# Threshold attention and a bilinear feed-forward layer: separate PSUM banks for scores in the first nine slots, and weight conversions split around the other work

## The chip, the cores and the metric

The kernel runs on one core of a Trainium2 chip. The metric is the device time of one execution in microseconds (us). A core has a matrix engine (PE, with its weight loads shown apart as PEld), three engines for elementwise work (DVE, ACT and POOL), and SP, which here only issues DMA transfers. Each works through its own list of instructions in order and waits for the others by semaphores. PE writes its results into PSUM, which this kernel uses as four pairs of banks; DVE and ACT read them from there.

## The reference

```python
scores = scale * np.matmul(q, k.transpose(0, 1, 3, 2))
thresh = np.max(scores, axis=-1, keepdims=True) - tau
scores = np.where(scores >= thresh, scores, -1000000000.0)
scores = scores - np.max(scores, axis=-1, keepdims=True)
attn = np.exp(scores)
attn = attn / (np.sum(attn, axis=-1, keepdims=True) + 1e-09)
x = concat_heads(np.matmul(attn, v))       # (8*576, 512)
...
a = x @ w_a
b = x @ w_b
return (a * b @ w_out).astype(np.float32)
```

There are 8 batches, 8 heads, 576 rows and a head width of 64; q, k and v are float32. The feed-forward part (below: ffn) has 4608 rows, width 512 and inner width 1536. Its three weight matrices arrive as 64-bit floats, 18.9 MB in all, and the kernel turns them into float32 itself.

## The kernel before, in words

**Slots.** The attention is cut into 160 units of up to 128 query rows for a pair of heads: `(i, u)`, pair `i` and row tile `u`, where `u = 4` is the tail of 64 rows of both heads. The program is a written-out loop over slots `g` (L756 to L837). Slot `g` computes the scores of unit `g` (`scores`, L314), their row maxima (`mx`, DVE L332), a bias (POOL L334) and a threshold (POOL L336), the exponentials (ACT L364), the masked product with its row sums (DVE L367), and the reciprocals (L376 to L380). Between these it places work of earlier units, of the weights and of the ffn. `keep_order` (L38) pins the order of emission on every engine, so what is written earlier in a slot runs earlier on its engine.

**The first eight units** (`BY_PE = 8`) are pairs 0 to 3 with row tiles 0 and 1. They are normalised and transposed on PE: `diagonals` (L388) makes a diagonal matrix `dg` of the reciprocals on ACT, and `turn_pe` (L396) in the next slot multiplies by it, in one large product (L406, evacuated by ACT L408) and a small one (L412, evacuated by DVE L414). In slots 2 to 9 `weighted_unit` (L499) multiplies with `v` (`pv`, L479), joins the two halves (ACT L468, DVE L469) and copies them for the ffn (POOL L489). In slots 0 to 2, q and k of the next pair are transposed on PE and copied out by DVE (L312). Later units are normalised on ACT (L386), transposed on DVE (L433, L446) and sent through DRAM (L441, L453, L464).

**Weights.** There are 36 pieces of 128 x 512 words of 64 bits (12 each for `wa`, `wb` and `wo`). `load_weights` (L193) has SP load them, at most `RAWS = 4` into work buffers and some more into the still unused `sums_u` space. Each then goes through two ACT instructions (L225, L226, `convert_first`), a POOL clamp (L232), and in the next slot a DVE sign (L238), a DVE shift (L246) and a POOL add (L251). `early[g]` lists the pieces whose first part is in slot `g`: two for slots 0 to 3, three for slots 4 to 9, two for slots 10 to 14. All signs, all shifts and all adds of a slot are placed together ahead of the masked products.

**The ffn** is a generator (`ffn`, L553) that goes through blocks of 256 rows. A block takes 24576 columns of moving data for `a` and `b` (L578, groups named `pab`, evacuated by ACT L584 for `a` and DVE L586 for `b`) and 12288 for the output (L665, or fewer by L621 once sums of weights are ready); 36864 in all is `BLOCK_COLS`. `advance(cols)` (L699) emits that many columns and may stop in the middle of a group, whose PSUM pair then stays taken. A planner sets `cols` per slot: `PACE_EARLY * BLOCK_COLS` up to slot 8, later what the backlog needs before the next block arrives, which is at slot 20 for the second block. In slots 0 to 8 it is all emitted at the slot's end, after the conversions; later in four portions. The first block has to wait for its rows and for `state["converted"]`, which must be 8, 16 and 24 before its inner steps 0, 2 and 4 (each step is two groups).

**PSUM.** `banks` (L125) takes any free pair of the four. The `h` buffers hold both the ffn's products and `dg`; the `osb` buffers hold the low parts of pieces in conversion.

Of the kernel before, what the change touches and what calls it, by code (L numbers as in the profile page):

```python
# [10 lines left out]
FP32 = mybir.dt.float32  # L11
# [11 lines left out]
PV_LAG = 4  # L23
# [6 lines left out]
CATCH_UP = 0.05  # L30
PACE_EARLY = 0.04
ROOM = 1024
# [19 lines left out]
def kernel(  # L52
# [62 lines left out]
    def pool(name, bufs, **kw):  # L115
        return ctx.enter_context(tc.tile_pool(name=name, bufs=bufs, **kw))
# [5 lines left out]
    scratch = pool("scratch", 3, space=bass.MemoryType.DRAM)  # L122
    psum = pool("psum", 4, space=PSUM)

    def banks(n, name):  # L125

        return psum.tile([P, 2, 512], FP32, tag="banks", name=name)[:, :, 0:n]

# [55 lines left out]
    raws, stages, extra, taken = {}, {}, [], {}  # L184
    state = {"loaded": 0, "converted": 0, "rows": 0, "sums": False, "through": 0, "over": False}

# [61 lines left out]
    def convert_add(n):  # L248
        if n in stages:
            top, low = pieces[n][0].bitcast(I32), stages.pop(n).bitcast(I32)  # L250
            nc.gpsimd.tensor_tensor(top, top, low, op=ALU.add)  # L251
            state["converted"] += 1

# [134 lines left out]
    def diagonals(i, u):  # L388

        ws, rcp = weights[i, u]  # L390
        dg = work.tile([P, 2, P], FP32, tag="h", bufs=H_BUFS, name="dg")
        for j in range(2):
            nc.scalar.activation(dg[:, j], ident, AF.Copy, scale=rcp[:, j:j + 1])
        weights[i, u] = (ws, dg)
# [88 lines left out]
    def x_tile(name):  # L483
        return work.tile([P, HP, HALF], FP32, tag="xT", bufs=XT_BUFS, name=name)
# [14 lines left out]
    def weighted_unit(i, u):  # L499

        b, hp = pairs[i]
        pv = product(turned.pop((i, u, "pe")), loaded[i]["v"], P)
        if (b, 0) not in x_of:
            x_of[b, 0] = x_tile("xT")
            state["xs"] = x_tile("xS")
        join(x_of[b, 0][:, hp, u * P:(u + 1) * P], pv[:, 0], pv[:, 1])
        exchange(x_of[b, 0], state["xs"], hp, u * P, (u + 1) * P, nc.gpsimd)
        if hp == HP - 1:
            state["rows"] = u + 1
            if u == 0:  # L510
                blocks.append(((x_of[b, 0], state["xs"]), ("first", b, 0)))

# [186 lines left out]
    def advance(cols):  # L699
        running["owed"] += cols  # L700
        while running["owed"] > 0:
# [13 lines left out]
            else:  # L715
# [4 lines left out]
                running["room"] = min(ROOM, whole // 2)  # L720

    def make_room():

        while running["rest"] and not (running["done"] >= running["room"] <= running["rest"]):
            owed = running["owed"]
            running["owed"] = 0.0
            advance(1)
            running["owed"] += owed - 1
# [7 lines left out]
    for i in range(0, NPR, HP):  # L736
# [7 lines left out]
    arrivals = [g + PV_LAG + 1 for g, (i, u) in enumerate(units)  # L744
                if i % HP == HP - 1 and part(i, u) and (i >= HP or u == NT - 1)]
    first = {i: g for g, (i, u) in enumerate(units) if u == 0}

    for name in ("q", "k"):
        prep_copy(*prep_pe(0, name))
    early = {}  # L750
    n = 0
    for g in range(NPIECES):
        size = min(3 if 4 <= g < 10 else 2, NPIECES - n)
        early[g] = list(range(n, n + size))
        n += size
    for g in range(len(units) + PV_LAG):  # L756
        written = len(pending)
        here = g < len(units)
        converting = bool(early.get(g)) or bool(early.get(g - 1))
# [4 lines left out]
        exchange_blocks()  # L764
        pace = (PACE if g > BY_PE else PACE_EARLY) * BLOCK_COLS
        if g > BY_PE:
            pace = min(pace, backlog() / (min([a for a in arrivals if a > g] + [len(units) + PV_LAG + 1]) - g))
# [4 lines left out]
        if g < 3:  # L772
            prep_copy(*prep_pe(g + 1, "q"))
        for n in early.get(g - 1, []):
            convert_sign(n)
        for n in early.get(g - 1, []):
            convert_shift(n)
        for n in early.get(g - 1, [])[-1:] + early.get(g - 1, [])[:-1]:
            convert_add(n)
        if g == 3:  # L780
            for c in range(0, NSUM - 2 * CW + 1, 2 * CW):
                extra.append(sums_u32[:, c:c + 2 * CW].rearrange("p (f w) -> p f w", w=2))
        load_weights(RAWS)
        if g > BY_PE and g <= len(units):
# [3 lines left out]
        if here:  # L788
            weigh(i, u)
        if 0 < g <= BY_PE:  # L790
            turn_pe(*units[g - 1])
# [13 lines left out]
        for n in early.get(g, [])[:1]:  # L805
            convert_first(n)
            convert_clamp(n)
        if here:
            reciprocal(i, u, nc.scalar if converting else nc.vector)
        if here and g < BY_PE:  # L810
            diagonals(i, u)
        elif here:
            normalise(i, u)
        for n in early.get(g, [])[1:]:
            convert_first(n)
            convert_clamp(n)
        load_weights(RAWS)
        for p in range(HP, NPR):
# [57 lines left out]
```

## Time and profile before

| what | value |
|---|---|
| median of 3 runs | 1483.64 us (1479.65 to 1484.49) |
| profiled execution | 1480.79 us, of which the span from first to last instruction is 1478.9 us |
| PE, PEld busy | 1425.3 us (96%), 1201.8 us (81%) |
| DVE, ACT, POOL busy | 925.8, 669.7, 360.1 us |
| first `sc` matmul of slots 0 to 4 | 11.79, 18.44, 26.44, 36.03, 43.17 us |
| ... of slots 5 to 10 | 49.47, 61.29, 70.65, 79.71, 90.87, 103.73 us |
| ... of slots 11 to 16 | 112.93, 122.50, 129.84, 138.74, 147.49, 157.16 us |
| ... of slots 17 to 20 | 164.14, 171.13, 176.39, 182.91 us |

The busy share of PE is taken from modelled ends of pipelined matmuls[...]. The starts of slots are read from the timeline of PE: the first `sc` matmul of each unit. A wait in the timeline stands in square brackets behind an instruction: how long its engine was idle before it, and whose end released it. The figure behind "x" is the number of records; a float32 matmul has two records here, so one inner step of the ffn over 64 rows of weights has eight.

### The profile page before, as it was taken

Reading aid. Unit: us, or ns where it says so; the run is one execution under the profiler, and the core shown is the slowest. Engines: PE = TensorE matmul, PEld = TensorE weight load, DVE = VectorE, ACT = ScalarE, POOL = GpSimd, SP = SyncE. Lnnn points to the kernel's source line nnn. Section 1 sums busy time; section 2 is a strip of 40 time slices with the busy share of each in tenths; the row PEclk is TensorE's granted clock in tenths of the full one; section 3 lists DMA queues with packets and bytes.
Section 4 is the critical chain, followed back from the end, with each engine's and each line's share of the span. In section 5 each row is a group of like instructions: output and inputs, shape, how many; then the busy total and the mean of one; then the engine's idle time right before and its main releaser. Section 6 shows DMA issues by size and latency. Waiting matters only on the chain.

```text
span 1478.9 us, 57127 instructions
## 1 busy us (share of the span) xinstructions
PE 1425.3 (96%) x25344; PEld 1201.8 (81%) x25344; DVE 925.8 (63%) x2068; ACT 669.7 (45%) x1213; POOL 360.1 (24%) x563
## 2 busy tenths in 40 slices
PE   5777999999999999999999999999999999999998
PEld 4666587898879898898888788889888888888886
DVE  5767677778767776675645766577756766622212
ACT  4766355555544554553533544355444554411010
POOL 3876522204030312122222213130404040310000
PEclk9999999999999999999999999999999999999999
DMA  9957888789868976786547876588756976530000
GB/s 192 214 154 184 169 168 191 175 178 194 209 139 169 193 174 144 176 184 163 125 118 137 183 164 150 119 188 184 158 138 138 193 174 158 135 90 16 2 17 16
DMA packets 624582, 220.75 MB, mean 149 GB/s; under 512 B 542928, under 2 KB 612048, under 8 KB 624336
## 3 DMA queue, kind: packets, MB, share of 16 engines
q1 hardware_dynamic: 621968, 216.52, 66.8%
q8 instruction: 199, 3.26, 0.9%
q10 hardware_dynamic: 2368, 0.59, 0.2%
q14 instruction: 47, 0.39, 0.1%
HBM read 127.40 MB, written 89.65 MB: 147 GB/s over the span
## 4 chain that ended last, share of the span: by engine, by line
PE 86%; DVE 5%; DMA 3%; ACT 2%; SPq 2%; issue 1%; POOL 1%; ACTq 0%; DVEq 0%; POOLq 0%
PE pab L578 47%; PE po L621 19%; PE sc L325 10%; PE pv L479 10%; PE po L665 1%; DVE tw L433 1%; DVE low L238 1%; DVE mx L332 1%; DMA swap<-tw 1%; DVE tw L367 1%; DMA raw<-in_moe_w_b_dram 1%; SPq L206 1%; SPq L151 0%; SPq L441 0%; DMA sums_u<-in_k_dram 0%
## 5 line engine op out<-in xcount | busy, mean ns | idle before, releaser
L332 DVE TENSOR_REDUCE mx<-sc 128x1 f32<-128x576 f32 x288 | 205.1, 749 | 133.0 <-PE sc L325 122.2
L578 PE MATMUL pab<-xS,wa_sb 64*64 64x256 f32 (+1 forms) x3584 | 271.6, 371 | 0.9 <-POOL xS L489 0.9
L578 PE MATMUL pab<-xS,wb_sb 64*64 64x256 f32 (+1 forms) x3584 | 268.2, 372 | 0.0
L325 PE MATMUL sc<-kT,qT 64*64 64x288 f32 x2304 | 243.4, 413 | 19.2 <-DVE kT L312 8.1
L590 POOL TENSOR_TENSOR h<-h 128x256 f32<-128x256 f32 x168 | 117.4, 733 | 542.1 <-PE po L621 539.0
L578 PE MATMUL pab<-xT,wa_sb 64*64 64x256 f32 (+1 forms) x3200 | 237.6, 371 | 5.3 <-POOL thr L336 2.1
L578 PE MATMUL pab<-xT,wb_sb 64*64 64x256 f32 (+1 forms) x3200 | 235.2, 368 | 5.6 <-DVE h L586 4.1
L621 PE MATMUL po<-wo_sb,h 64*64 64x256 f32 x3264 | 240.1, 376 | 0.0
L386 ACT ACTIVATE tw<-tw,rcp 128x576 f32<-128x576 f32 x244 | 176.1, 768 | 130.1 <-DVE rcp L380 129.9
L364 ACT ACTIVATE tw<-sc,bias,scalars 128x576 f32<-128x576 f32 x260 | 214.7, 832 | 38.3 <-POOL bias L334 25.4
L578 PEld LDWEIGHTS pab<-xS,wa_sb 64*64 64x64 f32 x3584 | 192.4, 133 | 31.3 <-POOL xS L489 5.3
L367 DVE SCALAR_TENSOR_TENSOR tw<-sc,thr,tw 128x576 f32<-128x576 f32 x260 | 203.6, 802 | 20.7 <-ACT tw L364 19.8
L578 PEld LDWEIGHTS pab<-xS,wb_sb 64*64 64x64 f32 x3584 | 193.6, 134 | 25.2 <-issue 0.8
L621 PEld LDWEIGHTS po<-wo_sb,h 64*64 64x64 f32 x3264 | 176.0, 132 | 24.8
L578 PEld LDWEIGHTS pab<-xT,wa_sb 64*64 64x64 f32 x3200 | 170.4, 134 | 30.4 <-DVE kept L469 4.3
L578 PEld LDWEIGHTS pab<-xT,wb_sb 64*64 64x64 f32 x3200 | 169.6, 133 | 27.9 <-DVE h L586 4.5
L479 PE MATMUL pv<-wT,vm 64*64 64x320 f32 (+3 forms) x2592 | 187.2, 381 | 3.1 <-ACT h L584 1.6
L325 PEld LDWEIGHTS sc<-kT,qT 64*64 64x64 f32 x2304 | 143.3, 135 | 52.5 <-issue 14.4
L621 PE MATMUL po<-sums_u,h 64*64 64x256 f32 x2448 | 180.6, 376 | 0.0
L433 DVE STREAM_TRANSPOSE tw<-tw 128x576 f32<-128x576 f32 x240 | 171.6, 753 | 0.2 <-ACT tw L386 0.2
L586 DVE TENSOR_TENSOR h<-h,pab 128x512 f32<-128x512 f32 (+1 forms) x112 | 73.3, 655 | 147.9 <-PE pab L578 140.1
L479 PEld LDWEIGHTS pv<-wT,vm 64*64 64x64 f32 x2592 | 141.6, 135 | 26.3 <-issue 2.8
(85 smaller groups left out, 1236.9 us busy)
## 6 DMA issues: line engine op xcount, KB each, us to landing
swap<-tw SPq DMA_DIRECT2D x240, 288.0 KB, 5.2
wT<-swap SPq DMA_DIRECT2D x28, 1440.0 KB, 7.8
wT<-swap SPq DMA_DIRECT2D x32, 1152.0 KB, 6.3
vm<-in_v_dram SPq DMA_DIRECT2D x32, 288.0 KB, 4.8
qT<-in_q_dram SPq DMA_DIRECT2D x112, 72.0 KB, 3.6
kT<-in_k_dram SPq DMA_DIRECT2D x112, 72.0 KB, 5.1
swap<-wt SPq DMA_DIRECT2D x112, 72.0 KB, 2.7
out_dram<-kept SPq DMA_DIRECT2D x30, 256.0 KB, 4.5
```

Of the source, the lines that this page charges most:

```text
L206: engine.dma_start(dst, part)
L325: nc.tensor.matmul(sc[j if u < NT else 0][to, c], qT[r, q0:q0 + D], kT[r, c * SH:(c + 1) * SH], start=True, stop=True)
L332: nc.vector.tensor_reduce(mx[:, c], sc[j], axis=AX.XY, op=ALU.max)
L364: nc.scalar.activation(wb[j], sb[j], AF.Exp, bias=bias[:, j:j + 1], scale=e_scale)
L367: nc.vector.scalar_tensor_tensor(out=wv, in0=sb[j], scalar=thr[:, j:j + 1], in1=wv, op0=ALU.is_ge, op1=ALU.mult, accum_out=sums[:, j:j + 1])
L386: nc.scalar.activation(w, w, AF.Copy, scale=rcp[:, j:j + 1])
L433: nc.vector.transpose(w, w)
L479: nc.tensor.matmul(pv[j * D:(j + 1) * D, r], vm[rows, k0], wT[rows, k0], start=(s == (NT if j == r else 0)), stop=(s == NT - 1))
L578: nc.tensor.matmul(pab[c * D:(c + 1) * D, r], w[rows, f // n, k, fs + c * D:fs + (c + 1) * D], moving, start=(k == 0), stop=(k == H - 1))
L586: nc.vector.tensor_tensor(ht, ht, pab, op=ALU.mult)
L590: (nc.vector if state["over"] else nc.gpsimd).tensor_tensor(*a, **kw)
L621: nc.tensor.matmul(po[c * D:(c + 1) * D, r, y], ht[rows, t0:t0 + D], other[rows, f], start=(f == 0), stop=(f == NF // 2 - 1))
```

## The change

- **Banks.** The four pairs get a tag each. Up to slot 8 (`state["apart"]`) scores alternate over pairs 0 and 1, and everything else over pairs 2 and 3, where one that an unfinished ffn group holds is left out. From slot 9 on all four are taken strictly in turn.
- **Conversions.** `convert_rest(g, k)` does sign, shift and add of one piece. Piece 0 of the slot before stays ahead of the masked products, piece 1 follows the normalisation, and piece 2 follows the ffn part (in slots up to 8). The `converted` counter the ffn looks at is that of the end of the previous slot.
- **Order.** In slots up to 8 the ffn part comes before the first halves of pieces 1 and 2, and `finish_group` carries it on to the end of its group. The reciprocal of the first eight units is placed straight behind the masked products, wholly on DVE.
- **Sizes.** Three pieces per slot from slot 4 to the end, so the last first half is in slot 13. `PACE_EARLY` is 0.06. From slot 9 on at most two pieces are loaded into work buffers. `dg` comes from the `osb` buffers. The changes in `weighted_unit` and `arrivals` give the same order of work for these units.

```diff
-PACE_EARLY = 0.04
+PACE_EARLY = 0.06
...
-    psum = pool("psum", 4, space=PSUM)
+    psum = pool("psum", 1, space=PSUM)
+
+    state = {"loaded": 0, "added": 0, "converted": 0, "rows": 0, "sums": False, "through": 0, "over": False,
+             "apart": True, "own": 1, "other": 1, "bank": 3, "last": 3, "held": None}
     def banks(n, name):
-        return psum.tile([P, 2, 512], FP32, tag="banks", name=name)[:, :, 0:n]
+        if state["apart"]:
+            own = name == "sc"
+            state["own" if own else "other"] ^= 1
+            if not own and 2 + state["other"] == state["held"]:
+                state["other"] ^= 1
+            m = state["own"] if own else 2 + state["other"]
+        else:
+            m = state["bank"] = (state["bank"] + 1) % 4
+        if name in ("pab", "po"):
+            state["last"] = m
+        return psum.tile([P, 2, 512], FP32, tag=f"banks{m}", name=name)[:, :, 0:n]
...
-            state["converted"] += 1
+            state["added"] += 1
...
-        dg = work.tile([P, 2, P], FP32, tag="h", bufs=H_BUFS, name="dg")
+        dg = work.tile([P, 2, P], FP32, tag="osb", bufs=OSB_BUFS, name="dg")
...
+    def finish_group():
+        left = None
+        while running["rest"] and running["left"] != left:
+            left, owed = running["left"], running["owed"]
+            running["owed"] = 0.0
+            advance(1)
+            running["owed"] += owed - 1
+        state["held"] = state["last"] if running["rest"] else None
...
+    def convert_rest(g, k):
+        for n in early.get(g - 1, [])[k:k + 1]:
+            convert_sign(n)
+            convert_shift(n)
+            convert_add(n)
...
-        size = min(3 if 4 <= g < 10 else 2, NPIECES - n)
+        size = min(2 if g < 4 else 3, NPIECES - n)
...
+        state["converted"] = state["added"]
+        if g == BY_PE + 1:
+            state["apart"], state["bank"] = False, state["last"]
+        if g == BY_PE + 2:
+            running["owed"] = 0.0
...
-        for n in early.get(g - 1, []):
-            convert_sign(n)
-        for n in early.get(g - 1, []):
-            convert_shift(n)
-        for n in early.get(g - 1, [])[-1:] + early.get(g - 1, [])[:-1]:
-            convert_add(n)
+        convert_rest(g, 0)
...
-        load_weights(RAWS)
+        load_weights(RAWS if g < 9 else 2)
...
             weigh(i, u)
+        if here and g < BY_PE:
+            reciprocal(i, u, nc.vector)
...
-        if here:
-            reciprocal(i, u, nc.scalar if converting else nc.vector)
         if here and g < BY_PE:
             diagonals(i, u)
         elif here:
+            reciprocal(i, u, nc.scalar if converting else nc.vector)
             normalise(i, u)
+        convert_rest(g, 1)
+        if g <= BY_PE:
+            advance(pace)
+            finish_group()
+        convert_rest(g, 2)
         for n in early.get(g, [])[1:]:
             convert_first(n)
             convert_clamp(n)
-        load_weights(RAWS)
+        load_weights(RAWS if g < 9 else 2)
...
-        advance((PORTIONS[2] if g > BY_PE else sum(PORTIONS[:3])) * pace)
-        advance(PORTIONS[3] * pace)
+        if g > BY_PE:
+            advance(PORTIONS[2] * pace)
+            advance(PORTIONS[3] * pace)
```

More of the change, by code (lines that the diff above doesn't have):

```diff
@@ L184 @@
     raws, stages, extra, taken = {}, {}, [], {}
-    state = {"loaded": 0, "converted": 0, "rows": 0, "sums": False, "through": 0, "over": False}
     NSUM = NF // 2 * 3 * CH
@@ L502, in weighted_unit @@
         pv = product(turned.pop((i, u, "pe")), loaded[i]["v"], P)
[L503 to L508, printed above, removed]
+        h, c0 = u // 2, u % 2 * P
+        if (b, h) not in x_of:
+            x_of[b, h] = x_tile("xT"), x_tile("xS")
+        x, xs = x_of[b, h]
+        join(x[:, hp, c0:c0 + P], pv[:, 0], pv[:, 1])
+        exchange(x, xs, hp, c0, c0 + P, nc.gpsimd)
+        if hp == HP - 1 and h == 0:
             state["rows"] = u + 1
             if u == 0:
-                blocks.append(((x_of[b, 0], state["xs"]), ("first", b, 0)))
+                blocks.append(((x, xs), ("first", b, 0)))
+        if hp == HP - 1 and u == NT - 1:
+            blocks.append(((x, xs), ("half", b, h)))
     def weighted(i, h):
@@ L743 @@
             units += [(p, u) for p in range(i, i + HP) for u in (2, 3, NT)]
-    arrivals = [g + PV_LAG + 1 for g, (i, u) in enumerate(units)
+    arrivals = [g + (PV_LAG if g >= BY_PE else 2) + 1 for g, (i, u) in enumerate(units)
                 if i % HP == HP - 1 and part(i, u) and (i >= HP or u == NT - 1)]
@@ L764 @@
         exchange_blocks()
-        pace = (PACE if g > BY_PE else PACE_EARLY) * BLOCK_COLS
-        if g > BY_PE:
+        pace = (PACE if g > HP * 2 else PACE_EARLY) * BLOCK_COLS
+        if g > HP * 2:
             pace = min(pace, backlog() / (min([a for a in arrivals if a > g] + [len(units) + PV_LAG + 1]) - g))
```

## The prediction

> **What bounds the kernel now.** I read the page's busy shares and slices first: PE is 96% busy, but its first four slices stand at 5 to 7 tenths. Then the table of stages.
>
> ```profile
> core 0: us, PE busy (x) PEld busy (x) DVE busy (x) ACT busy (x) POOL busy (x), PEclk, DMA share, GB/s
> 0.00:157.00 157.00, 116.32 (x2116) 95.91 (x2120) 107.94 (x238) 99.03 (x185) 100.52 (x142) 0.92 0.81 183
> ...
> 400.00:600.00 200.00, 198.10 (x3515) 174.34 (x3509) 137.94 (x315) 99.31 (x179) 48.33 (x77) 1.00 0.76 168
> ```
>
> From 157 us on (slot 16) PE has almost no gaps: in each 200 us up to 1400 it is busy 198 to 200. Work kept from PE before 157 us is never caught up, so the end moves by what the start of slot 16 moves. Up to then no engine is full: DVE, POOL and ACT are each busy 99 to 108 of 157 us and PE 116. The time lies in waits between them, so next came the timeline of all engines in slots 8 and 9.
>
> ```profile
> 80.86 0.66 ACT L226 ACTIVATE low<-sums_u 128x512 f32<-128x512 uint32 x1
> 81.42 0.35 ACT L584 COPY h<-pab 128x256 f32<-128x256 f32 x1
> 81.83 0.70 PE L325 MATMUL sc<-kT,qT 64*64 64x288 f32 x4 [0.98 <-ACT h L584]
> ...
> 88.05 0.44 PE L412 MATMUL tp<-dg,tw 128*64 128x128 f32 x4 [1.22 <-ACT wT L408]
> ...
> 93.28 0.35 ACT L584 COPY h<-pab 128x256 f32<-128x256 f32 x1
> ...
> 93.68 1.20 PE L479 MATMUL pv<-wT,vm 64*64 64x128 f32 x34 [1.61 <-ACT h L584]
> ...
> 100.36 1.10 PE L578 MATMUL pab<-xT,wb_sb 64*64 64x128 f32 x32 [2.67 <-DVE h L586]
> ```
>
> Two of the eight score products of slot 8 stop until ACT has evacuated an ffn group (L584), which stands behind four conversions on ACT. The small transpose product waits for the large one's evacuation: scores hold two pairs, a half-done ffn group a third, one is left. In slot 9 `pv` and then the ffn wait the same way. The POOL timeline shows how full that engine is, and that a 128x2 operation can take 0.30 us or five times that:
>
> ```profile
> 55.03 1.54 POOL L336 TENSOR_SCALAR thr<-mx,scalars 128x2 f32<-128x2 f32 x1
> ...
> 64.26 0.30 POOL L336 TENSOR_SCALAR thr<-mx,scalars 128x2 f32<-128x2 f32 x1
> 67.65 2.53 POOL L251 TENSOR_TENSOR wb_sb<-wb_sb,low 128x512 int32<-128x512 int32 x2 [1.70 <-DVE wb_sb L246]
> 70.14 1.29 POOL L251 TENSOR_TENSOR wa_sb<-wa_sb,low 128x512 int32<-128x512 int32 x1
> ```
>
> **What the Trainium skill says.** "Perfetto Trace Analysis", Optimization Strategy: repeated bubbles on the engine that should be full can mean that PSUM or SBUF lacks room for the next tile. The L412 row agrees; the wait of 1.22 us recurs at 67.83, 76.89 and 88.05. "PSUM — Partial Sum Buffer", Engine vs sequencer instructions: the queues of ScalarE, VectorE and GpSimd are strict FIFO and matmuls start and end in program order. So it is at 81.42. "SBUF — State Buffer", Who interferes with whom: a VectorE instruction with two SBUF inputs, or in a two-port mode, locks GpSimd out. The two `thr` rows fit it: 1.54 us beside DVE signs and shifts (54.28 to 57.2), 0.30 otherwise. The change leaves those instructions in being, so I allow 0.4 us per slot for it.
>
> **The change, part by part.** An ffn inner step over 128 columns takes 0.875 us per 32 records (L578 at 105.67, 106.55, 107.42), that is four steps, 512 columns: 1.71 ns a column. A half-width group is 1024 columns, 1.75 us.
>
> *Slots 5 and 8.* The planner's columns rise from 0.04 x 36864 + 576 - 640 = 1411 to 0.06 x 36864 + 576 - 640 = 2148, and `finish_group` rounds that up to three groups. Slot 5 does three; slot 6 only one, since step 2 needs 16 pieces and the counter, now a slot late, has 11 then and 14 in slot 7, which does none; slot 8 (17) does three. Seven groups in place of 5644 / 1024 = 5.5. On PE slot 5 is scores 1.2 + `pv` 1.2 + transposes 2.05 + 0.44 + three groups 5.25, and some 0.6 for the ACT evacuation (L408) before the first group: 10.7 us. Scores of the next slot wait for no group any more. The late conversions on ACT (4 x 0.57 = 2.3 us) run beside the next scores (1.2) and maximum (0.7) and bias (0.3); without that cover they would cost 2.3.
>
> *Slots 6 and 7.* PE has 5 to 7 us, ACT 7.5, DVE 7.4; POOL is longest: adds 2.53 + 1.29, clamps 3 x 0.62, bias and threshold 0.9, copies 1.3 = 7.9, plus the 0.4: 8.3 us. The next bias queues behind the last two clamps, and the exponentials wait for it; DVE has piece 0 (0.64 + 0.34 us) to do meanwhile.
>
> *Slot 9.* The waits of 1.61 and 2.67 us go, since no group is open and ACT's group copies come before its conversions. DVE: maxima 1.42, join 0.25, three pieces 3.0, transposes 1.35, products 1.5, ffn and small ones 0.6 = 8.1; POOL 8.3; with a hop I take 9.0.
>
> Slots 5 to 9 together: 10.7 + 8.3 + 8.3 + 10.7 + 9.0 = 47.0 against 103.73 - 49.47 = 54.3: **-7.3 us**. The 1.5 groups done ahead (2.6 us of PE) I count at nothing: the planner spreads the first block up to slot 20 anyway. Were PE the limit in slots 10 to 15, they would be a gain.
>
> *Slots 1 to 4* (31.0 us). One sign and shift (1.0 us) now stand behind the masked products, and in slots 1 to 2 behind the copy of k that the next scores wait for; the add of 1e-9 moves from ACT, behind conversions, to DVE (0.16 in place of 0.20 and two hops of 0.25). DVE is otherwise full in slot 4. Some 0.5 + 1.2 + 0.6 + 0.2: **-2.5 us**. With two pairs for the five other products, each waits only for the second last one's evacuation. Bounds 0 and -4.
>
> *Slots 10 to 15* (53.4 us). Slots 10 to 12 get one more first half each (ACT 1.15, POOL 0.62), and 11 to 13 one more second half (DVE 1.0, POOL 1.27): I take +1.0 in all, since the masked products no longer queue behind three pieces. Slots 14 and 15 lose two second halves each but one: -3. Sum **-2**, bounds +5 and -6. SP's loads: fewer in flight (2 plus the four in `sums_u`), each issued at the sign of the piece six before, so about one slot of 9 us ahead against 3.9 to 7.0 us to landing. SP's swap transfers (4.4 us of issue) stand between; late pieces of `wo` need one issue of 0.33. I cost it at nothing; if that cover fails, a piece is some 2 us late.
>
> *Banks in turn, slot 9 on.* The trace has no row for it. Zero if the pair in turn is always free, else PE waits. At 604.85 scores start, their first pair is read to 611.04 (L367): 6.2 us. In turn it is needed after scores 1.0, a full group 3.46 and `pv` 2.4, 6.9 us. The margin is thin but positive: **+1 us**, bounds 0 and +20. It can't gain, as PE idles only 5 us there (the waits of PE after 200 us).
>
> `dg` from `osb`: five buffers for at most four live tiles, nothing.
>
> Sum: -7.3 - 2.5 - 2 + 1 = **-10.8 us**. The profiled span of 1478.9 becomes 1468, the execution 1470; the median lies 2.85 above the profiled execution, so I predict **1473 us**.
>
> **The rivals.** *Slower: the strict turn costs more than the start gains.* In 151 slots from slot 9 on, scores hold their pairs for about 6.2 us with 0.7 to spare. Where a short tail unit, a late DVE or an output group of 3072 columns that just ended meets its own pair, PE stops for some tenths, up to 1.5 us for an evacuation. From 15.3 / 151 = 0.10 us per slot on, the change is slower by over 0.3%; at 0.12 the time is 1473 - 1 + 18 = 1490. For: the pool of before may take any free pair and PE has no slack. Against: two groups between reuses are nearly always there. Chance 0.15. *Slower by late pieces:* in slots 9 to 13 three pieces come through six places, and six of them late by 2 us cost 12, with slots 10 to 13 at DVE's and ACT's limit (+5) it ends near 1487 to 1490. Chance 0.09.
>
> *No change:* The same DVE, POOL and ACT work remains, and if POOL's late clamps and port locks keep a slot of three pieces near 10 us, only the waits of slot 9 go: -3 us, 1481. For: 9.4 of 10 us of POOL in the stretch 50 to 60. Chance 0.14.
>
> *Larger gain:* slots 5 to 13 run at 8.5 us, 14 and 15 at 7: 76.5 + 14 = 90.5 against 107.7, with -2.5 ahead, -20 us: 1464. For: no engine has more than 8.3. Against: PE has 10.7 in two of them. Chance 0.12.
>
> **How the numbers follow.** The likeliest case, 6 to 16 us gained, has 0.50; its own range is 1468 to 1478. Some 0.3%, 4.5 us, is what this measurement can tell from no change. Faster: 0.50 + 0.12 = 0.62; same 0.14; slower 0.15 + 0.09 = 0.24. The range from 1461 to 1490 takes in most of the larger gain and half of the slower cases, and leaves out 0.05 below and 0.12 above.
>
> **What would show it.** Right: slot 10's first scores near 94 us in place of 103.73 and slot 16's near 146; no wait of scores for ACT L584 or of L412 for L408 up to slot 8; PE busy 198 of 200 us from 200 to 1400 as before. Wrong: new PE waits for DVE L367, `kept` or `osb` evacuations after 200 us (strict turn); ACT L225 waiting for DMA (late pieces); POOL full with 10 us slots (no change).

## The result, and the profile after

| | before | after |
|---|---|---|
| median | 1484.07 us (1479.65 to 1485.25, 4 runs) | 1591.89 us (1591.46 to 1595.04, 4 runs) |
| ratio to before | | 1.0737 [1.0711, 1.0763] |
| profiled span | 1478.9 us | 1589.3 us |
| PE busy, PEld busy | 1425.3, 1201.8 us | 1458.5, 1166.8 us |
| mean granted PE clock | 0.991 | 0.974 |

The kernel became 7.4% slower, where 1473 us was predicted. Lines in the changed file are 12 to 15 higher: `mx` L344, bias L346, exponentials L376, masked products L379, `tp` L418 and L424 with copies L420 and L426, joins L480 and L481, `pv` L491, `pab` L593 with evacuations ACT L599 and DVE L601, `po` L636, sign, shift and add L250, L258, L263.

First the table of stages of the kernel after, with the same columns as before (busy time and records of PE, PEld, DVE, ACT and POOL, then PE's granted clock, the DMA share, GB/s):

```profile
core 0: us, PE busy (x) PEld busy (x) DVE busy (x) ACT busy (x) POOL busy (x), PEclk, DMA share, GB/s
0.00:157.00 157.00, 111.70 (x2060) 92.97 (x2064) 116.56 (x238) 95.14 (x175) 96.29 (x139) 0.92 0.79 181
...
400.00:600.00 200.00, 178.12 (x3021) 139.38 (x3015) 121.40 (x274) 88.27 (x159) 33.98 (x56) 0.96 0.69 148
```

The start did not get denser: PE is busy 111.7 us of the first 157, before 116.3. And from 400 to 600 us, where of all the edits only the turn is still at work, PE is busy 178 of 200 us in place of 198, it works off 3021 records in place of 3515, and its clock is 0.96 in place of 1.00. Scores of slot 20 start at 190.82 us (before 182.91), so 7.9 us are lost up to there. From there to the end of the span it takes 1398.5 us against 1296.0: **102.5 of the 110.4 us are lost after slot 20**.

Next PE's list of waits from 200 us on; these are its six largest rows. Before, the sum of this list was below 6 us (2.1 us for `kept`, 2.0 for issue, and smaller ones).

```profile
PE po L636 <- DVE kept L481: 19.5, 6, 5.4
PE pab L593 <- ACT h L599: 15.9, 9, 3.1
PE pab L593 <- DVE h L601: 13.7, 4, 4.7
PE po L636 <- DVE sums L390: 9.4, 3, 3.9
PE pab L593 <- DVE kept L481: 5.6, 3, 4.2
PE po L636 <- DVE h L601: 4.0, 1, 4.0
```

The figures are the sum in us, the number of waits and the longest. In these rows 26 waits make 68 us, mean 2.6; the rest of the list is nine waits of `pv` (6.3 us) and two of scores (1.0 us). Every waiting group in the rows shown belongs to the ffn, and nearly every releaser is the evacuation of an ffn group: `h` of `pab`, `kept` of `po`. `DVE sums L390` is a 128x2 operation that can release no PSUM pair; where it is named, it only came last in time. The timeline of all engines at 350 us shows one of these waits:

```profile
350.11 1.42 DVE L445 STREAM_TRANSPOSE tw<-tw 128x576 f32<-128x576 f32 x2
351.05 0.83 ACT L376 ACTIVATE tw<-sc,bias,scalars 128x576 f32<-128x576 f32 x1
351.46 0.77 DVE L379 SCALAR_TENSOR_TENSOR tw<-sc,thr,tw 128x576 f32<-128x576 f32 x1
351.78 0.58 ACT L480 COPY kept<-po 128x512 f32<-128x512 f32 x1
352.17 0.81 DVE L379 SCALAR_TENSOR_TENSOR tw<-sc,thr,tw 128x576 f32<-128x576 f32 x1
352.90 0.77 DVE L309 STREAM_TRANSPOSE kT<-kT 128x576 f32<-128x576 f32 x1
353.60 0.64 DVE L481 TENSOR_TENSOR kept<-kept,po 128x512 f32<-128x512 f32 x1
```

PE had ended the output group `po` at 349.4 us. Its evacuation is a copy on ACT and then an add on DVE. The copy stands behind the exponentials and starts 2.4 us later; the add stands behind swap transposes, masked products and a transpose of the next k, and ends at 354.2. The next `po` group is in the pair that this add has just read, and starts at 354.30. So one start in the pair of the group just ended costs not one evacuation (0.58 + 0.64 us) but all that ACT and DVE have queued ahead of it: 4.93 us.

The idle time is not all. Here is PE's own timeline after four waits (us from the start, duration of the group, and in brackets the wait and its releaser):

```profile
354.30 5.40 PE L636 MATMUL po<-wo_sb,h 64*64 64x256 f32 x48 [4.93 <-DVE kept L481]
441.37 2.82 PE L636 MATMUL po<-wo_sb,h 64*64 64x256 f32 x48 [1.81 <-DVE kept L481]
466.93 1.96 PE L593 MATMUL pab<-xT,wb_sb 64*64 64x256 f32 x32 [3.07 <-ACT h L599]
494.35 3.69 PE L593 MATMUL pab<-xT,wa_sb 64*64 64x256 f32 x32 [4.69 <-DVE h L601]
```

48 records of one shape take 2.82 us after a wait of 1.81, and 5.40 us after one of 4.93; 32 records of another shape take 1.96 us after 3.07 and 3.69 after 4.69. The table of stages after the first of these waits has PE's clock in its third column from the right:

```profile
354.30:358.00 3.70, 3.70 (x36) 2.26 (x40) 0.18 (x2) 1.44 (x2) 0.72 (x1) 0.50 0.90 202
358.00:362.00 4.00, 4.00 (x60) 2.36 (x59) 0.27 (x1) 0.00 (x0) 1.45 (x2) 0.77 1.16 281
362.00:366.00 4.00, 4.00 (x80) 2.65 (x76) 3.81 (x7) 2.12 (x5) 0.59 (x1) 1.00 0.60 99
```

PE runs at half clock for about 5.5 us (3.7 at 0.50, then 4 at a mean of 0.77), which costs another 2.8 us. The Trainium skill states in "TensorE: Matmul & The Clock Gate", Part 1, that the clock falls to half after an idle window of about 3.4 us and returns after as long a busy one. The trace agrees on the length: after slot 20, and until PE has done its work, half clock comes 13 times, for 3.41 us or twice that. It does not agree that PE has to be idle all that time: half clock follows a wait of 2.00 us (ended at 973.78 us), and none follows one of 3.07 (ended at 466.93). These are the steps of 3.41 us around the two:

```profile
462.25:465.66 3.41, 1.61 (x28) 0.92 (x20) 3.26 (x8) 2.78 (x7) 0.00 (x0) 1.00 0.87 239
465.66:469.07 3.41, 2.14 (x40) 1.58 (x44) 1.94 (x7) 2.59 (x4) 0.00 (x0) 1.00 0.98 351
...
970.85:974.25 3.40, 1.40 (x27) 0.81 (x21) 3.36 (x7) 2.89 (x6) 0.00 (x0) 1.00 0.98 322
974.25:977.66 3.41, 3.41 (x36) 2.10 (x32) 1.28 (x6) 0.00 (x0) 0.00 (x0) 0.50 0.29 107
```

In this profile the clock changes only at the ends of such steps. The wait of 2.00 us lies within one step, and PE is busy for 0.41 of it (1.40 of 3.40 us); the wait of 3.07 us is cut in two, and PE is busy for 0.47 and 0.63 of its two steps. In the two profiles with the strict turn (this one and e2 below), from slot 20 on, all 26 falls to half clock follow a step in which PE was busy for at most 0.42, and no step with 0.43 or more is followed by one. Half clock lasts on after steps with up to 0.72 busy and ends after steps with 0.80 or more. In the first twenty slots the profiles don't separate so cleanly.

The sum: from 200 us to the end PE is idle 81.7 us of 1389.3, before 12.0 of 1278.9, so 69.7 us more idle; and it is busy 1307.6 us in place of 1266.9, 40.7 more. Of these, 7.9 us are work that now falls after 200 us because slot 20 is late. The rest, 33 us, is the same matmuls taking longer. By the clock's record, half clock while PE is busy makes 26 us of it (before: none after slot 20). The other 7 us come without half clock: run e3 below has none after slot 20, and PE is still busy 8.6 us longer there than in the kernel before. 70 + 33 makes the 102.5 us.

### The profile page after: what moved, and what is told of

It is laid out like the page before. It is cut to its first block, busy times and chain, and to the rows that moved or that the text cites. A ratio compares the mean times of both kernels' runs of the same rounds, so it can differ in the third digit from the quotient of the medians.

```text
span 1589.3 us, 57034 instructions
## 1 busy us (share of the span) xinstructions
PE 1458.5 (92%) x25344; PEld 1166.8 (73%) x25344; DVE 939.8 (59%) x2077; ACT 668.4 (42%) x1204; POOL 356.3 (22%) x563
## 4 chain that ended last, share of the span: by engine, by line
PE 74%; DVE 11%; ACT 4%; SPq 3%; DMA 2%; issue 2%; POOL 2%; DVEq 0%; POOLq 0%; ACTq 0%
PE pab L593 42%; PE po L636 16%; PE pv L491 8%; PE sc L337 7%; SPq L156 2%; DVE tw L379 2%; DVE mx L344 2%; PE po L680 1%; DVE tw L445 1%; DMA kT<-in_k_dram 1%; ACT tw L398 1%; DVE kept L481 1%; DVE low L250 1%; ACT tw L376 1%; SPq L453 1%
## 5 line engine op out<-in xcount | busy, mean ns | idle before, releaser
L344 DVE TENSOR_REDUCE mx<-sc 128x1 f32<-128x576 f32 x288 | 205.2, 749 | 188.5 <-PE sc L337 176.4
L593 PE MATMUL pab<-xS,wa_sb 64*64 64x256 f32 (+1 forms) x3584 | 273.5, 375 | 1.8 <-POOL xS L501 1.0
L636 PE MATMUL po<-wo_sb,h 64*64 64x256 f32 x3264 | 242.3, 395 | 32.9 <-DVE kept L481 19.5
L593 PE MATMUL pab<-xT,wa_sb 64*64 64x256 f32 (+1 forms) x3200 | 240.3, 380 | 30.8 <-DVE h L601 13.7
L593 PE MATMUL pab<-xS,wb_sb 64*64 64x256 f32 (+1 forms) x3584 | 264.2, 372 | 0.0
L593 PE MATMUL pab<-xT,wb_sb 64*64 64x256 f32 (+1 forms) x3200 | 234.2, 374 | 23.7 <-ACT h L599 21.5
L337 PE MATMUL sc<-kT,qT 64*64 64x288 f32 x2304 | 238.9, 413 | 15.1 <-DVE kT L324 8.2
L376 ACT ACTIVATE tw<-sc,bias,scalars 128x576 f32<-128x576 f32 x260 | 214.5, 831 | 52.8 <-POOL bias L346 45.4
L636 PEld LDWEIGHTS po<-wo_sb,h 64*64 64x64 f32 x3264 | 164.8, 139 | 76.4 <-issue 26.6
L593 PEld LDWEIGHTS pab<-xS,wa_sb 64*64 64x64 f32 x3584 | 188.0, 136 | 39.8 <-POOL xS L501 5.3
L379 DVE SCALAR_TENSOR_TENSOR tw<-sc,thr,tw 128x576 f32<-128x576 f32 x260 | 203.4, 802 | 20.9 <-ACT tw L376 17.6
L593 PEld LDWEIGHTS pab<-xT,wa_sb 64*64 64x64 f32 x3200 | 164.1, 136 | 64.7 <-DVE h L601 15.6
L593 PEld LDWEIGHTS pab<-xS,wb_sb 64*64 64x64 f32 x3584 | 185.5, 134 | 31.6 <-issue 2.8
L593 PEld LDWEIGHTS pab<-xT,wb_sb 64*64 64x64 f32 x3200 | 160.8, 135 | 56.0 <-ACT h L599 25.6
L491 PE MATMUL pv<-wT,vm 64*64 64x320 f32 (+3 forms) x2592 | 182.5, 381 | 11.2 <-DVE h L601 6.6
L601 DVE TENSOR_TENSOR h<-h,pab 128x512 f32<-128x512 f32 (+1 forms) x112 | 73.4, 656 | 172.9 <-PE pab L593 168.4
L636 PE MATMUL po<-sums_u,h 64*64 64x256 f32 x2448 | 174.4, 377 | 0.0
L337 PEld LDWEIGHTS sc<-kT,qT 64*64 64x64 f32 x2304 | 138.3, 135 | 48.7 <-DVE kT L324 9.1
L491 PEld LDWEIGHTS pv<-wT,vm 64*64 64x64 f32 x2592 | 133.1, 134 | 41.2 <-DVE h L601 10.0
```

The source lines that it names most:

```text
L337: nc.tensor.matmul(sc[j if u < NT else 0][to, c], qT[r, q0:q0 + D], kT[r, c * SH:(c + 1) * SH], start=True, stop=True)
L344: nc.vector.tensor_reduce(mx[:, c], sc[j], axis=AX.XY, op=ALU.max)
L376: nc.scalar.activation(wb[j], sb[j], AF.Exp, bias=bias[:, j:j + 1], scale=e_scale)
L379: nc.vector.scalar_tensor_tensor(out=wv, in0=sb[j], scalar=thr[:, j:j + 1], in1=wv, op0=ALU.is_ge, op1=ALU.mult, accum_out=sums[:, j:j + 1])
L491: nc.tensor.matmul(pv[j * D:(j + 1) * D, r], vm[rows, k0], wT[rows, k0], start=(s == (NT if j == r else 0)), stop=(s == NT - 1))
L593: nc.tensor.matmul(pab[c * D:(c + 1) * D, r], w[rows, f // n, k, fs + c * D:fs + (c + 1) * D], moving, start=(k == 0), stop=(k == H - 1))
```

## The experiments: the loss after slot 20

In PE's order of work a group or a `pv` starts 27 times in the pair of the ffn group that ended just before it (14 times `pab` after `pab`, 10 times `po` after `po`). It comes about when two scores and one `pv` are handed out while a group is open, so that the turn has gone once around. 24 of these starts lie after slot 20. Each of them waits, from 0.7 to 5.4 us, 66.7 us together, and no other start there waits longer than 1.2 us. The other three (6.53, 1.42 and 1.43 us, at 151.06, 173.32 and 188.99 us) lie before it; together they are more than the 7.1 us by which slot 20 starts later than in e4, the same order of work with free pairs.

**Run e1_free_from_9.** The changed kernel, with any free pair from slot 9 on.

```diff
...
-            m = state["bank"] = (state["bank"] + 1) % 4
+            return pools["late"].tile([P, 2, 512], FP32, tag="banks", name=name)[:, :, 0:n]
...
         if g == BY_PE + 1:
             state["apart"], state["bank"] = False, state["last"]
+            early_pool.close()
+            pools["late"] = pool("psum_late", 4, space=PSUM)
```

> The changed kernel, with one edit: from slot 9 on any free PSUM pair is taken again, as in the kernel before, in place of the strict turn; every engine has the same instructions in the same order as in the changed kernel. Theory A (the strict turn makes ffn groups wait from slot 9 on): 1484 to 1493 us, PE busy over 197 of 200 us from 200 us on, and slot 20 at or below 186 us since the wait of 6.5 us in slot 14 goes as well. Rival B (the loss comes from the new order of work, which shifts how ffn groups lie against the slots): 1580 to 1595 us, as the changed kernel.

Measured: 1487.03 us (1482.49 to 1490.98), ratio 1.0047 [1.0023, 1.0071]. From slot 20's scores to the end 1294.2 us, as before (1296.0), and PE is again full:

```profile
400.00:600.00 200.00, 198.10 (x3529) 174.66 (x3523) 136.91 (x311) 98.54 (x178) 43.90 (x71) 1.00 0.77 171
```

The order of every engine's instructions is that of the changed kernel. So the turn is the cause of the loss after slot 20, and the new order of work is not. One forecast of theory A failed: slot 20 starts at 194.14 us in this profile and not by 186. Slot 9, up to which nothing differs from the changed kernel, already starts 8.3 us later than there.

**Run e2_before_turn_from_9.** The kernel before with this one edit: pairs in turn from slot 9 on, and the ffn group that is open at that point ended first.

```diff
...
+        if "late" not in pools:
+            return pools["early"].tile([P, 2, 512], FP32, tag="banks", name=name)[:, :, 0:n]
+        m = state["bank"] = (state.get("bank", 3) + 1) % 4
+        return pools["late"].tile([P, 2, 512], FP32, tag=f"banks{m}", name=name)[:, :, 0:n]
```

> The kernel before, with the strict turn over the four pairs from slot 9 on; to start it, the open ffn group is finished at the end of slot 8. Theory A: 1560 to 1595 us, PE waits of 3 to 6 us for evacuations by DVE L469, ACT L584 and DVE L586 between 200 and 1400 us. Rival B: 1482 to 1490 us.

Measured: 1589.54 us (1588.41 to 1593.95), ratio 1.0754 [1.0726, 1.0782]. PE's waits from 200 us on are those of the changed kernel, to within 0.1 us (lines are those of this kernel):

```profile
PE po L624 <- DVE kept L472: 19.5, 6, 5.4
PE pab L581 <- ACT h L587: 15.8, 9, 3.1
PE pab L581 <- DVE h L589: 13.7, 4, 4.7
```

The edit alone makes up the whole loss.

**Run e3_turn_skip_own.** The changed kernel in turn, but the pair of the last ffn group is left out.

```diff
-            m = state["bank"] = (state["bank"] + 1) % 4
+            m = (state["bank"] + 1) % 4
+            if m == state["last"]:
+                m = (m + 1) % 4
+            state["bank"] = m
```

> The changed kernel, with one edit: from slot 9 on the turn leaves out the pair that the last ffn group had, and takes the one after it. Counted in the order of PE, 27 groups or products start in the pair of the ffn group that has just ended, since two scores and a pv came between. Theory A1 (these 27 starts, each waiting for a whole evacuation in the queues of ACT and DVE, are the cost): 1484 to 1505 us. Theory A2 (many small waits for pairs that scores still hold): over 1560 us. Rival B: 1580 to 1595 us.

Measured: 1514.68 us (1512.32 to 1518.02), ratio 1.0244 [1.0223, 1.0266]. This lies between the two theories, 10 us above the range of A1 and far below that of A2. Without the 27 starts in the own pair, 77 of the 109 us between the turn and free pairs (run e4) are gone. From slot 20 on the kernel takes 1321.1 us, still 25 more than before. The largest waits left are of another kind, as this kernel's list from 200 us on shows (lines are 3 higher again):

```profile
PE pab L596 <- DVE tw L382: 6.6, 16, 1.2
PE pab L596 <- DVE sums L393: 3.8, 7, 0.5
```

Sixteen waits of 0.4 us for the masked products, which hold the scores' pairs: leaving one pair out brings the turn around sooner and eats the thin margin that the prediction had worked out. None of the waits after slot 20 brings half clock here; of the 25 us, 16.5 are idle time and 8.6 longer busy time. The strict turn's own list has no wait of this kind, so there the margin held, and its loss is that of the own pairs.

**Run e4_free_all.** The changed kernel with any free pair in all slots (`pool("psum", 4)`, one tag).

> The changed kernel with the pool of before in all slots: any free pair from the start, no pairs for scores alone; the order of instructions on every engine is that of the changed kernel. Theory A: within 8 us of the run with free pairs from slot 9 on. If pairs for scores alone are worth what the prediction said for slots 5 to 9, this run is 2 to 6 us slower than that one and scores wait for ACT evacuations again; if they are worth nothing, within 1.5 us.

Measured: 1482.64 us (1479.53 to 1487.52), ratio 1.0023 [1.0014, 1.0032]. All other edits of the change together bring nothing, where the prediction had -11.8 us for them. This is the second error, and it has its own runs. Separate pairs for scores in the first nine slots are no gain either: e1, which keeps them, is 4.4 us slower than e4, where a gain of 2 to 6 us or no difference was expected. The two ratios' intervals overlap, so that a loss isn't shown.

## The experiments: the first twenty slots

In all these runs any free pair is taken in every slot; the row of the changed kernel stands beside them for comparison. The table gives the length of the stages, from the first `sc` matmul of each slot in the profiled execution; "start" is slot 20's.

| kernel | slots 1-4 | 5-9 | 10-15 | 16-19 | start | ratio to before |
|---|---|---|---|---|---|---|
| before | 31.0 | 54.3 | 53.4 | 25.8 | 182.91 | 1 |
| after | 28.3 | 56.3 | 59.3 | 28.8 | 190.82 | 1.0737 |
| e4 free pairs | 28.3 | 52.2 | 60.1 | 24.9 | 183.69 | 1.0023 [1.0014, 1.0032] |
| e5 two pieces from slot 10 | 28.4 | 53.0 | 52.8 | 27.0 | 179.58 | 0.9978 [0.9970, 0.9987] |
| e6 conversions together | 35.3 | 57.9 | 55.0 | 26.4 | 192.78 | 1.0062 [1.0045, 1.0079] |
| e7 ffn at the end | 28.7 | 53.4 | 52.1 | 26.5 | 178.88 | 0.9953 [0.9935, 0.9970] |
| e9 = e5 and e7 | 28.7 | 50.7 | 52.9 | 26.9 | 177.13 | 0.9969 [0.9954, 0.9984] |
| e10 = e9, add on ACT | 29.1 | 52.3 | 51.8 | 26.6 | 177.69 | 0.9973 [0.9961, 0.9985] |
| e12 = e9, split to slot 9 | 28.1 | 51.5 | 53.5 | 27.0 | 178.58 | 0.9976 [0.9964, 0.9988] |
| e8 before, early reciprocal | 35.6 | 58.9 | 52.4 | 25.7 | 190.73 | 1.0063 [1.0048, 1.0078] |
| e11 before, split | 28.8 | 58.6 | 52.7 | 27.4 | 185.15 | 1.0013 [1.0001, 1.0025] |

From slot 20 on every kernel with free pairs needs 1294 to 1298 us. One and the same program can differ in slots 1 to 8 by several us from one execution to another. The changed kernel, e1 and e3 issue the same instructions up to slot 9, yet it starts at 93.73, 102.06 and 96.85 us, and slots 1 to 4 take 28.3, 32.3 and 29.4 us. So a stage of one profile counts only beside the ratio, and differences of a few us in a single row are not shown.

**Run e5_free_sizes**: `size = min(3 if 4 <= g < 10 else 2, ...)`, the sizes of before.

> The change with PSUM pairs from one pool of four, any free one taken (1482.6 us), and with the piece sizes of before (three pieces in slots 4 to 9 only, else two). Theory P (the third piece in slots 10 to 12 costs time, since DVE's shifts collide there with POOL's adds): slots 10 to 15 go from 60 us back towards 54, and the time is 1477 to 1479. Rival Q (the third piece costs nothing, the splitting itself does): 1481 to 1484, slots 10 to 15 stay at 58 to 61.

Measured: 1478.38 us (1475.15 to 1481.65). The time and the 52.8 us of slots 10 to 15 are as theory P expects.

**Run e7_free_ffn_end**: in the first nine slots the ffn steps are at the slot's end again, at the pace of before, no group is finished ahead, and the columns still owed at slot 10 are kept.

```diff
-PACE_EARLY = 0.06
+PACE_EARLY = 0.04
...
-            advance(pace)
-            finish_group()
...
+        advance((PORTIONS[2] if g > BY_PE else sum(PORTIONS[:3])) * pace)
+        advance(PORTIONS[3] * pace)
```

> The change with PSUM pairs from one pool of four, any free one taken (1482.6 us), with the early ffn steps at the end of the slot behind the late conversions again, at the pace of before (0.04) and with no group finished ahead. Theory F (three whole groups in slots 5 and 8 hold up the next scores and set PE idle ahead of them): slots 5 and 8 go from 15.8 to 11 to 13 us, and slot 20's scores come 2 to 4 us earlier, time 1479 to 1481. Rival (the groups are work that has to be done somewhere before slot 20): slots 5 and 8 are shorter, the others longer by as much, time 1481 to 1484.

Measured: 1474.90 us (1471.91 to 1478.90), the fastest of all, and 4 us below the range of theory F. Slots 5 and 8 fall from 15.0 and 15.1 to 10.4 and 11.0 us, but slots 6, 7 and 9 become longer by as much, as the rival had said; its time, 1481 to 1484, was wrong too. The gain appears elsewhere: slots 10 to 15 take 52.1 us, with the three pieces that P had made responsible. So P is not the cause by itself either: each of the two edits alone takes away the same 7 to 8 us of this stage. The stage from slot 10 to 15 in e4, and then in e7, shows what they have in common:

```profile
98.70:158.80 60.10, 48.30 (x909) 38.73 (x913) 51.49 (x94) 34.95 (x61) 40.16 (x49) 0.89 0.66 170
```

```profile
100.25:152.39 52.14, 43.50 (x957) 35.86 (x953) 49.82 (x91) 34.22 (x59) 39.30 (x47) 1.00 0.74 194
```

In e4 PE needs 48.3 us for 909 records, in e7 43.5 for 957: the clock is 0.89 in the one and 1.00 in the other, 0.97 in e5. Of the 8 us, 4.8 are longer busy time and 3.2 are idle. DVE is busy 49.8 of e7's 52.1 us, but its load is not what sets the length: in e12 it is busy 45.1 us and the stage takes 53.5. In e4 half clock begins four times there, behind waits of PE of 2.1, 1.8, 2.0 and 4.0 us for four different things (the last is scores that wait for the masked products). In e7 PE waits for at most 2.0 us, and no half clock follows. Why the waits of e4 fall as they do, and which of them decides, wasn't tried.

**Run e6_free_together**: signs, shifts and adds together ahead of the masked products again.

> The change with PSUM pairs from one pool of four, any free one taken (1482.6 us), and with all signs, shifts and adds of a slot together ahead of the masked products again, as in the kernel before. Theory Q (the split costs: shifts run beside POOL's adds and clamps and are then 0.6 to 0.9 us in place of 0.42, and the next maxima wait behind them): the mean shift goes back to 0.42 to 0.45 us, slots 10 to 15 to 54 to 56, and the time is 1476 to 1479. Rival P (the third piece costs, wherever it stands): slots 10 to 15 stay near 60, time 1481 to 1485, and slots 1 to 4 lose their 2.7 us.

Measured: 1490.43 us (1487.11 to 1492.77), above both ranges. Theory Q is wrong in its sum and right in its part: the shifts are back at 415 to 445 ns and slots 10 to 15 at 55.0 us, but slots 1 to 9 lose 12.7 us against e4. **Run e8_before_rcp** shows why.

```diff
             weigh(i, u)
+            if g < BY_PE:
+                reciprocal(i, u, nc.vector)
...
-        if here:
-            reciprocal(i, u, nc.scalar if converting else nc.vector)
         if here and g < BY_PE:
             diagonals(i, u)
         elif here:
+            reciprocal(i, u, nc.scalar if converting else nc.vector)
```

> The kernel before (1479.6 us) with one part of the change alone: in the first eight slots the add of 1e-9 and the reciprocal stand on DVE right behind the masked products. If this makes up what slots 1 to 4 gain in the change (2.7 us), slots 1 to 4 take 28.3 to 29 us in place of 31.0 and the time is 1476.5 to 1478. If the gain came from the split pieces or the two bank pairs, slots 1 to 4 stay at 30.5 to 31 and the time is 1479 to 1480.

Measured: 1490.32 us (1489.86 to 1491.56), above both ranges. In the place of a gain, slots 1 to 4 lose 4.6 us. The timeline of slot 1 in e8:

```profile
25.62 1.26 POOL L251 TENSOR_TENSOR wa_sb<-wa_sb,low 128x512 int32<-128x512 int32 x1
25.81 1.10 DVE L378 TENSOR_SCALAR sums<-sums 128x2 f32<-128x2 f32 x1
...
27.21 0.75 DVE L312 COPY kT<-tp 128x576 f32<-128x576 f32 x1
...
28.02 1.22 PE L325 MATMUL sc<-kT,qT 64*64 64x288 f32 x16 [1.88 <-DVE kT L312]
```

The add of 1e-9 over 128x2 elements takes 1.10 us beside POOL's add, which began ahead of it; they end together, at 26.9 us. Behind it on DVE stands the copy of k that the next scores wait for (25.62 us before, 27.21 here). The Trainium skill, "SBUF — State Buffer", Who interferes with whom, has a cause that fits: DVE and POOL share a pair of ports, a DVE `tensor_scalar` can be in a mode that needs it, and whichever of the two engines comes first has it for its whole instruction while the other is blocked. That this add is in such a mode isn't shown apart from its time. It is the same in all of slots 1 to 4: in e8 and in e6, which both have the early reciprocal without the split, these adds take 1.10 to 1.18 us, and in no profile with the split is one above 0.45. The prediction had used that section for POOL's small operations, and not for DVE's. In the changed kernel only one POOL add has been issued by then, and the same operation (24.58 us) takes 0.17.

**Run e11_before_split**: the kernel before with the second and third piece's sign, shift and add behind the reciprocal, by `convert_rest`.

> The kernel before with one part of the change alone: the signs, shifts and adds of a slot's second and third piece stand behind the masked products and the reciprocal in place of ahead of them. If the split is what gains in the early slots (the change without it loses 7 us in slots 1 to 4 and 6 us in slots 5 to 9, and wins 5 us in slots 10 to 15): 1474 to 1478 us in place of 1481, slots 1 to 9 shorter by 3 to 8 us. If it only pays together with the early reciprocal: 1480 to 1484 us.

Measured: 1482.72 us (1476.71 to 1488.50), ratio 1.0013, so no gain. The time is that of the case in which the split pays only with the early reciprocal, but e10 below has the split without it and is faster than the kernel before. In e11's profile slots 1 to 4 win 2.2 us and slots 5 to 9 lose 4.3. That the early gain comes from the split rests on more than this one profile: of the ten profiles with the split nine have 28.1 to 29.4 us in slots 1 to 4 (e1 has 32.3), and the two kernels with neither the split nor the early reciprocal, before and e2, have 31.0 and 30.2. **Run e10_rcp_on_act** is e9 with the add of 1e-9 on ACT again.

> As the run with free pairs, the split, two pieces from slot 10 on and the ffn steps at the slot's end, but with the add of 1e-9 on ACT behind the conversions again in the first eight slots. If the early reciprocal on DVE is a gain once the pieces are split (0.17 us and no hops to ACT and back): slots 1 to 4 go from 28.4 to 30 to 31 us, and the time is 1.5 to 3 us more. If the split alone makes slots 1 to 4 faster: they stay at 28 to 29 us, same time within 1 us.

Measured: 1476.71 us (1473.30 to 1482.15), ratio 0.9973 [0.9961, 0.9985], slots 1 to 4 29.1 us. With the split, it is the same on ACT or on DVE.

**Run e9_ffn_end_sizes**: e5's and e7's edits together.

> Free pairs in every slot, the split of signs and shifts and the early reciprocal kept, and both of the parts undone that cost alone: the ffn part ahead of the late conversions (1474.9 us without it) and the third piece from slot 10 on (1478.4 us without it, against 1482.6 with both). If the two costs lie in different slots and add up: 1470 to 1472 us, slot 20's scores at 174 to 177 us. If the same POOL and DVE work takes its room in either case: 1474 to 1478 us.

Measured: 1476.22 us (1473.24 to 1481.39). The gains do not add up, as they remove one and the same loss. **Run e12_split_to_9** is e9 with all signs and shifts together from slot 10 on.

> As the run with free pairs, the split, two pieces from slot 10 on and the ffn steps at the slot's end, but with all signs and shifts of a slot together ahead of the masked products from slot 10 on. If the split costs in slots 10 to 15 by the shifts that run beside POOL's adds of wo (mean 0.88 us in place of 0.42): shifts of wo back at 0.42 us, slots 10 to 15 shorter by 1 to 4 us and the time as much lower. If with two pieces that collision has room: the same time within 1.5 us.

Measured: 1476.75 us (1473.34 to 1479.37), ratio 0.9976 [0.9964, 0.9988]. The shifts of `wo` fall from a mean of 624 ns (e9) to 420, and it gives nothing: the shifts are slowed and have room.

e7, e9, e10 and e12 are all faster than the kernel before, by 0.2 to 0.5%, and their intervals overlap. They keep the split (e12 up to slot 9) and drop the bank plan and the early ffn part.

## Why the prediction was wrong

- **Banks in turn, slot 9 on: +1 us, bounds 0 and +20.** This step failed. It measured about +105 us (e1 against the changed kernel; e2: +110 on the kernel before). The step checked one reuse, the scores' pairs after 6.9 us, and found a margin; it didn't list which pair each group gets. The case that decides was named in the slower rival, the output group that meets its own pair. It was priced at "some tenths, up to 1.5 us for an evacuation", and it costs up to 5.4 us of wait, since the evacuation stands in two full queues, and up to 2.8 us of half clock behind it. The 102.5 us after slot 20 are 4.3 us for each of the 24 such starts there, and 14 of the 27 are `pab` after `pab`, which the rival had not named. The margin itself held. The argument "two groups between reuses are nearly always there" is what fell: two scores and a `pv` handed out while a group is open bring the turn back to that group's pair, with no group between.
- **The rival that strict turns cost more** had the right place and sign; its point of decision, 0.10 us per slot, was passed sevenfold (102.5 us over the 140 slots from slot 20 on, 0.73 each).
- **Slots 1 to 4: -2.5 us.** Right in this profile, -2.7, and in most of those with the split, but e3 and e1, with the same instructions, have -1.6 and +1.3. The term for the add of 1e-9 (0.16 us on DVE) is right only beside the split; alone that move costs 4.6 us (e8), and with the split it is worth nothing that can be measured (e10). What gain there is comes from the split.
- **Slots 6 and 7: 8.3 us each; slot 9: 9.0.** 7.8, 7.8 and 9.1, so right in this profile; e1 and e3 have 11.1 and 11.7 in slot 6 and 6.8 in slot 7, so that one by one the agreement is in part luck.
- **Slots 5 and 8: 10.7 us each.** Wrong: 15.8 and 15.9 (e1 13.8 and 19.5, e3 13.5 and 17.3). Slots 5 to 8 together take 47.2, 51.3 and 49.3 us in the three profiles, where 38.0 was predicted. The sum of PE's work assumed the full clock and the groups ready to start. The timeline of slot 5 after:

```profile
51.61 1.32 POOL L346 TENSOR_SCALAR bias<-mx,scalars 128x1 f32<-128x1 f32 x2
52.70 1.55 ACT L376 ACTIVATE tw<-sc,bias,scalars 128x576 f32<-128x576 f32 x2 [1.36 <-POOL bias L346]
54.15 1.07 ACT L420 COPY wT<-tp 128x512 f32<-128x512 f32 x2
55.32 1.01 PE L593 MATMUL pab<-xT,wa_sb 64*64 64x128 f32 x25 [3.17 <-POOL wa_sb L263]
```

  The bias stands behind two late clamps, the exponentials behind the bias, the evacuation of the transposes behind the exponentials, and the first ffn group behind that, since both pairs for other products are taken. (The evacuation ends at 55.22 us, POOL's add, which the profile names, at 55.25; the two can't be told apart here.) PE waits 3.17 us there, and the mean clock from 55.3 to 61.0 us is 0.70; the next scores stand behind all three groups. The 0.6 us that the prediction took for that evacuation was the term mis-sized: it measured 3.17, and the full clock assumed for the groups behind it was 0.70.
- **Slots 10 to 15: -2 us, bounds +5 and -6.** Wrong: +5.9 in the changed kernel, in which the turn already waits, and +6.7 with free pairs (e4), beyond the upper bound. The +1.0 us for one more piece in slots 10 to 12 was sized at the full clock; with the ffn part moved ahead as well, PE stays at a clock of 0.89 there. Either of e5's and e7's edits removes the loss, so it is neither part's by itself. DVE's slower shifts don't explain it: e7 has them and is the fastest, and taking them away (e12) gives nothing.
- **What would show it.** Slot 10 starts at 102.81 us and slot 16 at 162.07, not near 94 and 146. The waits of scores for the ffn evacuation and of L424 for L420 went, as predicted; the waits themselves weren't worth what the slots cost. Others came in their place, up to 93 us: scores wait three times for the masked products (5.7 us, longest 3.2), and two ffn groups wait 6.2 us. The first is no matter of separate pairs, as e4 has it too (5.8 us, longest 3.2). ACT L237 never waited for pieces up to slot 9: the rival of late pieces is not what happened.

What stays open: where the 7 us of longer busy time without half clock come from; which part of e5's and e7's edits ends the loss in slots 10 to 15; why the split alone (e11) loses in slots 5 to 9, if that is more than the spread of one program, while with the change's other small edits (e10: `dg` from other buffers, the later counter, fewer loads) it doesn't, and how much of the differences between e7, e9, e10 and e12 is more than chance.

## What to carry to other kernels

A pool that hands out buffers strictly in turn must be checked for its worst reuse, by writing out the sequence of owners: the one that meets its own last evacuation is the one to price, and its price is everything queued ahead of that evacuation on its engines, not the evacuation. On a full PE a stall costs its own length, and in this case from 2.0 to 3.1 us on, depending on where it fell, up to 2.8 us more at half clock. Before an operation is moved between engines, look at what the other engine that shares its port will have running at that time.

## What was not expected of the hardware

- Half clock costs show at single waits, at full load: 48 records of one shape took 2.82 us after a wait of 1.81 us, and 5.40 us after 4.93. After slot 20 it made 26 of the 102.5 us.
- What goes with half clock is not the length of a wait but PE's busy share in a step of 3.41 us: in two profiles, from slot 20 on, the clock fell after steps with at most 0.42 busy and never after steps with 0.43 or more, so a wait of 2.00 us did it and one of 3.07 did not.
- A DVE operation over 128x2 elements, 0.17 us alone, took 1.10 to 1.18 us beside one POOL add of 1.26 us; a DVE shift of 0.42 us had a mean of 0.88 us for `wo` in the changed kernel, where it ran beside adds and clamps.
